# Linear attention with a per-step decay, then a two-layer network, on one core: idle products, conversions and transposes placed anew in rounds 0 and 1

## Chip, core and metric

The kernel runs on one core of a Trainium2 chip. The metric is the time of the program on the device in microseconds (us), the median of several executions. Five engines take part: TensorE (PE, matrix products and transposes into PSUM), VectorE (DVE), ScalarE (ACT), GpSimd (POOL) and SyncE (SP, which issues most DMAs). Each follows its own list of instructions, in order, and waits on semaphores for the others.

## What is computed

Inputs r, k, v, w have the shape (4, 8, 768, 48): batch, heads, steps, width. For each batch and head a 48 by 48 state runs over 768 steps; the outputs of the heads are put side by side (width 384), normed, and sent through two dense layers with a residual.

```python
for t in range(S):
    cur = einsum('bhd,bhe->bhde', u[None] * kt, vt)
    y[:, :, t] = einsum('bhd,bhde->bhe', rt, state + cur)
    state = wt[:, :, :, None] * state + einsum('bhd,bhe->bhde', kt, vt)
x = y.transpose(0, 2, 1, 3).reshape(B, S, H * D)
mu = mean(x); var = mean((x - mu) ** 2)
xn = (x - mu) / sqrt(var + 1e-6) * g_ln
out = x + maximum(xn @ w_ch1, 0) @ w_ch2        # 384 -> 1536 -> 384
```

## The kernel before, in words

**Tiling.** The work is cut into 8 rounds, each one batch and one half of 384 steps. A round has two units of four heads; u0, u1 are the units of round 0, units 2 and 3 those of round 1, and so on. Inside a unit two heads stand on the partitions (a pair, `pr`), and steps are cut into chunks of 64.

**Attention in levels.** Within a chunk the decay between two steps is built up by doubling. There are six levels (`NLEV`). At level `lev`, `quads` (line 366) makes the level products a_ps (24 products of fp32, each two PE instructions, so 48 per unit), `grow` (386) multiplies blocks of r and k in place by decays (DVE, one operation for each of r and k), and `keep` (401) copies the wanted part of a_ps into A (DVE, predicated copies; after the last level ACT copies, run later by `finish`, line 423). `quads` of the next level reads what `grow` wrote. `turned` (276) transposes w, k or r of one pair: three PE transposes into one PSUM buffer (w_ps, k_ps, r_ps) and one ACT copy out (to wT, kT, rT). The buffers are those of pool `ps_t`, two in all, which `product_sums` (own_ps), `ends` (kn_ps) and `turned_x` (xT_ps) share in turn: a third user waits until the first one's copy on ACT is done. `totals` (293) makes products of decays on DVE. `products` and `product_sums` make each step's own term with u. After the levels `ends` transposes k, `states` makes kv on PE and runs the state over the chunks on DVE, and `outputs` makes y.

**The network's weights.** w_ch1 and w_ch2 come in 24 raw parts of 384 KB, and both are rewritten once. `fetch` asks for a raw part by DMA (four buffers). `begin` is the first half of a conversion: three ACT operations (into w_sb, and twice into a buffer "held" or "rest"), after which it fetches the next raw part. `join` is the second half, three DVE operations. Parts from 12 on have four rest buffers, which ACT writes and join frees.

**The network's products.** `mlp` (562) is a generator: a step is six PE instructions of 384 columns, either one h_ps with a relu on ACT or a part of o_ps. `fill(until, tasks)` (line 619) spreads a slot's tasks evenly between the MLP steps up to a running total. A slot is one level of one round, and its totals stand in `UNTIL`.

**Idle products.** `warm(n)` issues n products of zeros, 128 by 128 (named "idle"), into a PSUM buffer that nobody reads; each is two PE instructions.

**Order.** The names PE, ACT, DVE, POOL and SPO (lines 67 to 69) keep the program's order on their engines. So an ACT copy that stands behind a conversion in the program runs behind it, and a DMA on SPO behind those before it. Loads on plain SP may be placed by the scheduler.

**Round 0** (lines 648 to 721) is written out by hand: transposes of u0 and u1, level 0, loads of round 1 and of v, two conversions (`begin`, lines 669 and 670), then levels 1 to 5 (674 to 688) with the transposes of round 1 between them, nine PE transposes a level from level 2 on (list `ahead`). A third conversion stands in level 1 and a fourth in level 3. Three more come with `own_term`, `outputs` and `norm`, after the levels. **Round 1** (line 731 on, `rnd == 1`) has no attention of an earlier round to finish; it has the levels of units 2 and 3, the first MLP steps, 17 begins and 21 joins (`BEGINS`, `JOINS`, line 730), and the transposes of round 2 in slots 1 to 3. In its slot 5 joins and begins stand first among the tasks, then `ends` and `finish`.

## Time and profile before

| what | us |
|---|---|
| median of 11 runs | 601.7 |
| lowest, highest | 597.5, 604.92 |
| profiled execution, its own time | 602.64 |
| its span, first to last instruction | 600.9 |
| PE busy | 578.9 |
| DVE busy | 294.8 |
| ACT busy | 199.7 |
| mean granted clock of TensorE | 0.969 |

The profile is of one execution. The span runs from the first to the last instruction; the program's own time has 1.74 us more around it. Each group is a line of the program's helper that keeps the order (L49 everywhere), so groups are told apart by the tiles they read and write: "a_ps<-rT,kT" are level products. "Idle before" is the time an engine stood before a group, and the name behind the arrow is what it waited for. A granted clock of 0.50 means that TensorE ran at half speed in that stretch; a busy PE at half speed still counts as busy.

The conversions of round 0 on ACT, with the copies around them, as the timeline has them (start, duration in us, what):

| start | us | ACT |
|---|---|---|
| 16.50 | 0.90 | two copies of k of u1 |
| 17.29 | 3.19 | conversions 0 and 1, to 20.48 |
| 22.33 | 0.17 | copy of own_ps of u1 |
| 23.94 | 1.69 | conversion 2, after a wait of 1.44 for its raw part |
| 25.88 | 1.12 | two copies of w of unit 2 |
| 32.75 | 1.67 | conversion 3 |

### The profile page before, as it was taken

What the parts mean: (1) busy time and instruction counts of PE and PEld (TensorE: products, weight loads), DVE (VectorE), ACT (ScalarE), POOL (GpSimd) and SP (SyncE); (2) the same over time, 40 slices, a digit from 0 to 9 for tenths busy, and PEclk for the clock granted to TensorE, in tenths of its full rate; (3) what the DMA queues carried; (4) which work ended last, traced back from release to release, by engine and by line L of the source; (5) the groups of instructions that cost most, each with busy time, mean ns of one, the idle gap of its engine ahead of it and who ended that gap; (6) DMA issues with size and microseconds to landing.
All of it is one profiled execution on the core that took longest, in us unless ns stands there. A gap on an engine that the chain in (4) does not pass through costs nothing.

```text
span 600.9 us, 19140 instructions
## 1 busy us (share of the span) xinstructions
PE 578.9 (96%) x8550; PEld 395.1 (66%) x8550; DVE 294.8 (49%) x706; ACT 199.7 (33%) x430; POOL 70.0 (12%) x100
## 2 busy tenths in 40 slices
PE   8997979899999999999999999999999999999997
PEld 7887656566666766676666666667666666666554
DVE  3857968989546554435265344526245332130000
ACT  3547766812352215411343215321241015301200
POOL 5000000002170007000240007000230000000000
PEclk9659889999999999999999999999999999999999
DMA  9972697134432412132113402012000000000000
GB/s 158 191 181 76 159 231 181 52 66 89 89 62 51 95 38 41 34 78 59 32 24 61 94 16 54 1 32 58 15 2 4 15 14 14 2 14 26 0 14 26
DMA packets 122129, 36.82 MB, mean 61 GB/s; under 512 B 115776, under 2 KB 118976, under 8 KB 122048
## 3 DMA queue, kind: packets, MB, share of 16 engines
q1 hardware_dynamic: 119648, 35.31, 26.7%
q8 instruction: 67, 1.10, 0.8%
q10 hardware_dynamic: 2400, 0.30, 0.6%
q14 instruction: 14, 0.11, 0.1%
HBM read 28.51 MB, written 4.72 MB: 55 GB/s over the span
## 4 chain that ended last, share of the span: by engine, by line
PE 86%; ACT 5%; DVE 5%; issue 2%; DMA 1%; SPq 0%; DVEq 0%; ACTq 0%
PE h_ps L49 29%; PE o_ps L49 29%; PE a_ps L49 11%; PE y L49 4%; PE r_ps L49 2%; PE w_ps L49 2%; PE k_ps L49 2%; PE kv L49 2%; PE xT_ps L49 2%; PE kn_ps L49 2%; DVE w_sb L49 1%; PE own_ps L49 1%; ACT rest L49 1%; DVE A L49 1%; PE idle L49 1%
## 5 line engine op out<-in xcount | busy, mean ns | idle before, releaser
L49 PE MATMUL o_ps<-w_sb,h 128*128 128x384 f32 x576 | 199.5, 492 | 0.5 <-issue 0.5
L49 PE MATMUL h_ps<-xT,w_sb 128*128 128x384 f32 x576 | 197.7, 494 | 0.0
L49 PEld LDWEIGHTS h_ps<-xT,w_sb 128*128 128x128 f32 x576 | 107.0, 193 | 65.9 <-issue 2.1
L49 PEld LDWEIGHTS o_ps<-w_sb,h 128*128 128x128 f32 x576 | 105.4, 192 | 63.0 <-issue 2.9
L49 PEld LDWEIGHTS a_ps<-rT,kT 48*64 48x64 f32 x4608 | 78.4, 142 | 20.5 <-issue 15.7
L49 PE MATMUL a_ps<-rT,kT 48*64 48x32 f32 x4608 | 83.5, 226 | 7.3 <-issue 5.6
L49 ACT ACTIVATE h<-h_ps 128x384 f32<-128x384 f32 x96 | 46.5, 489 | 124.9 <-PE h_ps L49 124.8
L49 DVE TENSOR_TENSOR o<-o_ps,x 128x384 f32<-128x384 f32 x24 | 13.4, 557 | 133.5 <-PE o_ps L49 133.5
L49 POOL TENSOR_TENSOR vo<-v,own 128x576 f32<-128x576 f32 x12 | 14.3, 1195 | 366.5 <-DVE own L49 366.5
L49 DVE COPY_PREDICATED A<-mask,a_ps 128x384 f32<-128x384 int8 x80 | 54.4, 750 | 0.0
L49 DVE TENSOR_TENSOR rT<-rT,tot 128x384 f32<-128x384 f32 x80 | 45.6, 579 | 15.5 <-PE a_ps L49 15.5
L49 DVE TENSOR_TENSOR kT<-kT,tot 128x384 f32<-128x384 f32 x80 | 45.3, 567 | 10.7 <-PE a_ps L49 10.2
L49 DVE SCALAR_TENSOR_TENSOR s<-s,decay,kv 128x48 f32<-128x48 f32 x160 | 29.3, 258 | 28.1 <-PE kv L49 28.1
L49 DVE TENSOR_TENSOR x<-y,vo 128x288 f32<-128x288 f32 x32 | 13.2, 454 | 50.1 <-PE y L49 50.1
L49 ACT ACTIVATE xT<-xT_ps,g_sb 128x384 f32<-128x384 f32 x24 | 13.7, 580 | 58.6 <-PE xT_ps L49 58.5
L49 ACT COPY rT<-r_ps 128x384 f32<-128x384 f32 x32 | 14.4, 480 | 43.8 <-PE r_ps L49 43.8
L49 ACT COPY kT<-k_ps 128x384 f32<-128x384 f32 x32 | 14.8, 480 | 38.1 <-PE k_ps L49 38.1
L49 PEld LDWEIGHTS y<-v,A 64*64 64x64 f32 x384 | 20.9, 134 | 8.2 <-issue 6.0
L49 PE MATMUL y<-v,A 64*64 64x48 f32 x384 | 23.9, 222 | 0.8 <-DVE A L49 0.8
L49 PE MATMUL y<-vx,A 64*64 64x48 f32 x384 | 23.9, 222 | 0.0
L49 ACT COPY kn<-kn_ps 128x384 f32<-128x384 f32 x32 | 14.4, 480 | 28.3 <-PE kn_ps L49 28.2
L49 PE MATMUL y<-sx,rx 48*64 48x48 f32 x384 | 23.3, 219 | 0.0
(70 smaller groups left out, 551.9 us busy)
## 6 DMA issues: line engine op xcount, KB each, us to landing
raw<-in_moe_w_ch_dram SPq DMA_DIRECT2D x24, 384.0 KB, 4.0
nat_w<-in_w_dram SPq DMA_DIRECT2D x48, 96.0 KB, 2.9
nat_k<-in_k_dram SPq DMA_DIRECT2D x48, 96.0 KB, 2.9
v<-in_v_dram SPq DMA_DIRECT2D x48, 96.0 KB, 3.0
out_dram<-o SPq DMA_DIRECT2D x24, 192.0 KB, 1.9
nat_r<-in_r_dram SPq DMA_DIRECT2D x45, 96.0 KB, 3.0
vx<-v SPq DMA_DIRECT2D x32, 72.0 KB, 2.3
nat_r<-in_r_dram ACTq DMA_DIRECT2D x3, 96.0 KB, 3.9
```

Of the source, the lines that this page charges most:

```text
L49: return lambda *args, **kw: self.tc.keep_in_program_order(f(*args, **kw))
```

## The change

It does five things:

1. In round 0 it adds idle products: two before `product_sums(u0)`; two instead of one after r and after k of u1; three before level 1; two between the level products of u0 and u1 in level 1; and 3, 2, 1, 1, 3 at the end of the product part of levels 1 to 5, where only level 5 had two. That is 17 more.
2. It puts four conversions ahead of level 1, where two stood, and takes those of levels 1 and 3 away. The DMAs that they ask for (raw parts 4 and 5) now stand on SP before the loads of v, and parts 6 and 7 before those of vx.
3. In round 1 the begins of the six slots are 3, 2, 3, 3, 4, 2 (before 4, 3, 1, 3, 4, 2) and the joins 3, 3, 3, 3, 4, 5 (before 3, 3, 3, 4, 4, 4).
4. The transposes of round 2 are spread over slots 0 to 3 as 2, 4, 4, 2 pairs (before 0, 4, 6, 2), in the order w, k, r.
5. The new helper `mixed` spreads the begins, joins and transposes of a slot evenly over one list. That list is added at the end of the slot's tasks, so in slot 5 it comes after `ends` and `finish`. The total of MLP steps after slot 2 is 9 instead of 8.

```diff
+    def mixed(*lists):
+        return [
+            t for _, t in sorted(
+                (((i + 0.5) / len(l), t) for l in lists for i, t in enumerate(l)),
+                key=lambda at: at[0],
+            )
+        ]
...
     totals(0, DVE)
+    warm(2)
     product_sums(u0)
     for nm in "rk":
         run(each(turned, [u1], nm, pairs))
-        warm(1)
+        warm(2)
...
     load(new[1], eng=SPO)
-    run(each(load_v, [u0, u1], [SPO]) + each(load_vx, [u0, u1], [SPO]))
     begin()
     begin()
+    run(each(load_v, [u0, u1], [SPO]))
+    begin()
+    begin()
+    run(each(load_vx, [u0, u1], [SPO]))
+    warm(3)
     grow(u1, 0)
     keep(0, 0)
...
     for lev in range(1, NLEV):
-        for q in (u0, u1):
-            quads(q, lev)
+        quads(u0, lev)
+        if lev == 1:
+            warm(2)
+        quads(u1, lev)
         if lev == 1:
             product_sums(u1)
         else:
             run(ahead[3 * lev - 6 : 3 * lev - 3])
-        if lev in (1, 3):
-            begin()
-        if lev == 5:
-            warm(2)
+        warm((3, 2, 1, 1, 3)[lev - 1])
...
-    UNTIL = [3, 6, 8, 11, 14, 16, 19, 21, 24]
+    UNTIL = [3, 6, 9, 11, 14, 16, 19, 21, 24]
...
-    JOINS, BEGINS = (3, 3, 3, 4, 4, 4), (4, 3, 1, 3, 4, 2)
+    ahead = [t for nm in "wkr" for t in each(turned, units_of(2), nm, pairs)]
+    JOINS, BEGINS = (3, 3, 3, 3, 4, 5), (3, 2, 3, 3, 4, 2)
...
-                for i in range(max(JOINS[lev], BEGINS[lev])):
-                    tasks += [join] * (i < JOINS[lev]) + [begin] * (i < BEGINS[lev])
...
-            if new and first <= lev < first + 3:
-                due = each(turned, new, "wkr"[lev - first], pairs)
-                if rnd == 1 and lev == 2:
-                    due += each(turned, new[:1], "r", pairs)
-                if rnd == 1 and lev == 3:
-                    due = due[NP:]
-                tasks += due
+            if rnd > 1 and new and first <= lev < first + 3:
+                tasks += each(turned, new, "wkr"[lev - first], pairs)
...
+            if rnd == 1:
+                n = (1, 2, 2, 1, 0, 0)[lev] * NP
+                tasks += mixed([begin] * BEGINS[lev], [join] * JOINS[lev], ahead[:n])
+                del ahead[:n]
             fill(UNTIL[slot], tasks)
```

## The prediction

> **What bounds the kernel now.** I read the page first, then the granted clock in fine windows, then the timeline of each engine where the clock falls, and last the chain of waits.

> The page says that TensorE (PE) bounds the whole, and that the first slices differ from the rest:

> ```profile
> PE 578.9 (96%) x8550; PEld 395.1 (66%) x8550; DVE 294.8 (49%) x706; ACT 199.7 (33%) x430; POOL 70.0 (12%) x100
> PEclk9659889999999999999999999999999999999999
> ```

> From slice 7 on hardly anything but PE work counts, and the change doesn't touch it: whatever is won or lost in the first 125 us goes through to the end. In the first slices the clock is low though PE is busy. Windows put at the edges of the clock's steps show it (name, PE busy, PEld, DVE, ACT, POOL, clock, DMA share, GB/s):

> ```profile
> 20.62:44.50 23.88, 23.88 (x440) 20.97 (x439) 16.57 (x33) 9.58 (x20) 0.00 (x0) 0.50 0.84 192
> 58.17:65.00 6.83, 6.30 (x27) 4.62 (x27) 6.35 (x15) 3.54 (x7) 0.00 (x0) 0.50 0.73 159
> 78.65:82.06 3.41, 3.28 (x10) 2.35 (x11) 1.29 (x4) 1.41 (x4) 0.00 (x0) 0.50 1.02 335
> ```

> Half clock for 23.9 us: that is all of levels 2 to 5 of round 0. The timeline of PE there:

> ```profile
> 22.22 2.79 PE L49 MATMUL a_ps<-rT,kT 48*64 48x32 f32 x96
> 24.94 1.54 PE L49 MATMUL w_ps<-ident,nat_w 128*128 128x128 f32 x6
> 26.41 0.90 PE L49 MATMUL r_ps<-ident,nat_r 128*128 128x128 f32 x3
> 27.24 2.79 PE L49 MATMUL a_ps<-rT,kT 48*64 48x32 f32 x96
> ```

> A level takes 5.02 us of PE at half clock (2.72 for 96 level products, 2.30 for 9 transposes). VectorE (DVE) needs four growths at 0.48 apart and two predicated copies of about 0.47, 2.9 us, and waits ("1.76 <-PE a_ps" at 38.86). The other stretch is round 1:

> ```profile
> PE w_ps L49 <- ACT wT L49: 2.8, 1, 2.8
> PE a_ps L49 <- DVE s L49: 1.2, 1, 1.2
> ```

> At 75.99 the third w transpose needs a PSUM buffer whose copy stands on ScalarE (ACT) behind conversions: ACT is full from 66.1 to 79.1. PE idles 2.79, and the clock is then half for one window.

> [...] the steps stand at 20.62, 44.50, 58.17, 65.00, 78.65, 82.06 and 464.32, all multiples of 3.41 apart to within 0.03. So the phase differs from execution to execution; the 11 times spread over 7.4 us. [...] here window 78.65 to 82.06, half of it w transposes, raised it, so I count them. [...] "ACT own" at 22.33 stands where the program has it, before the third conversion. [...]

> **What the clock asks for (my estimate).** I weigh each product by the part of the array that it uses: two idle products of 128 columns took 0.22 us, so an a_ps product (32 columns, 48 by 64 of 128 by 128) counts 0.005 us, a call of quads (48) 0.24; a y or kv product 0.010; own_ps (2 columns) nothing; a transpose 0.125. Windows that ended in half clock: 17.20 to 20.62 (144 a_ps) 21%; 54.75 to 58.17 27%; 75.24 to 78.65 22%; the one before 464.32 29%. Windows that kept full clock: 47.90 to 51.30 35%, 51.30 to 54.75 39%. So the bound lies near a third. To come back, 79% (24.03 to 27.45 and 34.27 to 37.69) did not do and 96% (78.65 to 82.06) did.

> **The change part by part.**

> *Idle products.* 17 more: at 13.2 two (they lie beside the wait of own_ps for wT, 0.24: about 0.1 is late), one more each after r and k (0.22 each, the second behind k; the growth chain of u1 moves by about 0.3), three and two around the level-1 products, then 3, 2, 1, 1, and 3 instead of 2. Each costs 0.21 at full clock and 0.43 at half. The first aim is met: window 17.20 to 20.62 now holds 1.07 of idle products besides 0.8 of quads, about 56%, and full clock stays past 20.6.

> *Four conversions ahead of the levels.* Before, two stood there, the third after the copy of own, the fourth in level 3. ACT runs in order: the third needs raw part 2, and the fourth raw part 3. The SP queue is unchanged up to that fetch: part 2 was issued at 19.66 and landed at 23.94 (ACT's wait shows it), part 3 was issued at 21.2 and landed about 4.0 later, 25.2. So ACT stands from 20.5 to 23.94, converts until 25.6 and, at 1.56 a conversion, until 27.15; only then comes the copy of own_ps (0.17). own_ps holds one of the two ps_t buffers. In level 2, PE does its first w transpose in the other, and the second waits for this copy, with the r transpose, the idle products and level 3 behind it. With quads of level 2 done at about 24.3 (own_ps 20.7 to 22.2, three idle products, quads from 22.9), PE idles from 24.65 to 27.3. This is the wait of 75.99 at a new place. Window 24.03 to 27.45 then holds about 18%, and the clock falls after all, at 27.45 or (20.62 to 24.03 holds 30%) at 24.03.

> *Then the levels at half clock.* Second w transpose 27.3 to 28.0, r to 28.8, two idle products 0.85: quads of level 3 at 29.6 instead of 27.31, +2.3. Levels 3, 4 and 5 have 1, 1 and (3-2) more idle products at 0.43: +1.3. kn_ps begins at 46.8 instead of 43.23: **+3.6**. From there all recurs one clock window (3.41) later, so I add nothing. Bounds: if the clock returns in 37.69 to 41.10 (transposes plus idle products fill 87% there, between the two known values) this is +1.3; if the wait is bridged at full clock, see the first rival.

> *Raw parts ahead of v.* Parts 4, 5 are issued at 28.2 and 6, 7 after v, where they came at 35.9. Four took about 4.3 us of the DMA (38 to 42 at 252 to 396 GB/s). v lands at about 35.3, vx at about 41; kv needs v at 45.78 and y needs vx at 50.60. The slack covers it: nothing. Without it, it would be at most the 4.3. The w loads of round 2 behind them on SP move little.

> *Round 1.* Conversions are 3, 2, 3, 3, 4, 2 instead of 4, 3, 1, 3, 4, 2; the w transposes of the first unit come in slot 0. The first conversion of slot 0 now lies before the first relu, in ACT's idle 63.1 to 65.76. ACT per level is then about 7 us against 8 of PE: the 2.79 goes, with 1.7 of the 3.41 at half clock and some of 0.30, 0.19 and 0.41. What is late next: in slot 5 the kn transposes now stand ahead of all conversions and of the first MLP step. Before, o_ps 109.17 to 111.21 covered the growth of k (DVE 110.20 to 111.2). DVE's load is the same, and one join moves from slot 3 to slot 5. DVE by my count: level 2 begins at 80.65 instead of 84.08, level 3 at 89.1, level 4 at 96.0, the growth of k at 104.9 to 105.9 (before 110.2 to 111.2); PE ends its level-5 quads at about 103.2. So PE waits 2.7 there, after which the clock falls in most phases (1.7). Sum on PE from 62.28 to the a_ps of 120.17: 57.9, less waits of 4.9 and 1.7 of clock, is 51.3 of work; after, 51.3 + 2.7 + 0.3 + (0 to 1.7) = 54.3 to 56.0: a gain of 1.9 to 3.6. DVE, which ends its joins at 114.3 instead of 118.19, allows 3.9. I take **-2.8**.

> *Step 9 for 8 in UNTIL* moves one MLP step from slot 3 to 2: no work, in the sum above.

> Sum: 602.64 (the profiled execution; span 600.9) + 3.6 - 2.8 = 603.4; it lay 0.94 above the median of 601.7, so the median comes to 602.5.

> **Rivals.**

> 1. *Full clock through round 0.* If no window over the wait at 24.65 falls under a third, quads of level 3 start at 28.6, and a level takes about 2.9: kn_ps at 37.5, -6.0 with its own products at full clock. With -2.8 this is 593.8, median about 593. For: 56% in the first window. Against: 2.6 us idle of 3.41; by my weights only some 0.65 of 3.41 of the phases pass both windows.
> 2. *Half clock, but raised in level 4:* +1.3 - 2.8, median 600.2, or lower where it is raised in level 3: 598. For: 87% lies between 79 and 96; against: the window must hold the whole run of 2.73.
> 3. *The wait of round 1 moves to level 5 and gives all back (slower).* DVE's joins are the same 21, and the chain of waits over 101 to 118 is ACT conversions and DVE joins in turn. If DVE reaches the growth of k no earlier than 110, PE waits 5 where an o_ps step stood, and round 1 gives 0: 602.64 + 3.6 = 606.2, median 605.3. It decides from a wait of 4.9. Against: DVE idled 4.0 and 1.6 in levels 2 and 3, which earlier level products remove.

> **How the numbers follow.** Likeliest case 0.43, 602.5, its own range 600 to 604.6; rival 1 0.23; rival 2 0.14, half of it under 598.7; rival 3 0.20. A measurement here tells about 0.5% (3 us) from no change. Faster: 0.23 + 0.07 = 0.30; within: 0.43 + 0.07 = 0.50; slower: 0.20. The range 594 to 606 leaves out half of rival 1 and the tail of rival 3.

> **What would show it.** A PE wait "w_ps <- ACT" or the like of over 2 us at about 25 and ACT's own copy at about 27 show the block; a clock of 0.5 from about 27.4 to 48 and level products 5.4 apart show the half-clock levels. Clock 1.00 over 25 to 40 makes it wrong by 9 us. In round 1 the wait at 76 must be gone and one before kn_ps of about 2.7 be there; were it absent, round 1 gains a further 2 to 3.

## The result, and the profile after

The changed kernel takes 609.93 us (median of 12 runs, 606.65 to 614.62). The kernel before took 601.7 (47 runs beside them). The ratio is 1.0153 with a 95% interval of 1.0123 to 1.0183: slower by 1.5%, where 602.5 and "no change" were forecast. Medians are of all executions; ratios, and the means further down, leave out those that took over 1.5% more than the fastest of their kernel. The profiled execution of the changed kernel took 614.57 us, the second longest of the 12; its span is 612.8 and its mean clock 0.961 (before 602.64, 600.9, 0.969). So its profile shows more loss than the median has.

Busy times and the clock row of the page of the changed kernel, the counterparts of the two page lines shown of before:

```profile
PE 584.4 (95%) x8584; PEld 399.3 (65%) x8584; DVE 295.5 (48%) x706; ACT 198.9 (32%) x430; POOL 70.4 (11%) x100
PEclk9877899779999999999999999989999899999999
```

PE has 34 matrix instructions more (17 idle products of two) and 5.5 us more of busy time. Before, the clock row had its low digits, 6 and 5, in the second and third place; now there is no digit below 7, but 7 and 8 stand in two places, and 8 further on. Windows put at the edges of the clock's steps give the stretches (columns as in the windows of before):

```profile
20.00:25.50 5.50, 4.24 (x121) 3.84 (x117) 5.50 (x12) 1.95 (x4) 0.00 (x0) 1.00 1.01 228
25.50:35.70 10.20, 8.76 (x155) 7.92 (x157) 3.54 (x8) 4.13 (x10) 0.00 (x0) 0.50 0.81 180
42.60:46.00 3.40, 2.79 (x13) 2.82 (x14) 1.12 (x3) 0.96 (x2) 0.00 (x0) 0.50 0.33 63
52.80:63.00 10.20, 10.20 (x256) 9.82 (x256) 5.09 (x13) 4.64 (x11) 0.00 (x0) 0.50 0.32 87
...
107.40:114.20 6.80, 6.11 (x10) 3.20 (x10) 2.78 (x7) 3.64 (x8) 0.00 (x0) 0.50 0.26 72
127.90:134.70 6.80, 6.50 (x102) 4.87 (x103) 6.37 (x22) 1.72 (x4) 0.00 (x0) 0.50 0.01 4
```

With the window left out (66.5 to 69.9) the stretches at 0.50 up to 135 us are six, of together 40.8 us, against 34.1 in three before. Cut to 0.01 us, the stretches from step to step between 25.50 and 134.73 last 10.24, 6.83, 3.41, 6.83, 10.24, 3.41, 3.42, 37.54, 6.83, 13.65 and 6.83 us, each at 0.50 or at 1.00 throughout: multiples of 3.41 to within 0.03, as in the forecast's profile. A clock window is one length of 3.41 between such steps; that its filling decides on the clock behind it is the forecast's estimate. The first falls, at 25.50 here and at 20.62 before, are 4.88 apart, which is no multiple of 3.41. The level products of level 5 of round 0 and most of level 4's now run at full clock, but own_ps and y of round 0 (52.8 to 63.0) and two stretches around the end of round 1 do not.

The waits of PE (in total, number, longest; us):

```profile
PE o_ps L49 <- ACT h L49: 4.2, 1, 4.2
PE a_ps L49 <- issue: 3.8, 3, 1.7
PE w_ps L49 <- ACT own L49: 2.7, 1, 2.7
PE k_ps L49 <- DMA vx<-v: 2.6, 1, 2.6
PE a_ps L49 <- DVE s L49: 2.5, 1, 2.5
```

The wait of 2.8 for wT in round 1 is gone, as forecast. A wait for own is there, as forecast. The largest, 4.2 for h, was in no step of the forecast. Round 0 on the timeline of PE (start, duration, what, idle before and its releaser):

```profile
23.70 0.55 PE L49 MATMUL w_ps<-ident,nat_w 128*128 128x128 f32 x3
26.94 0.90 PE L49 MATMUL w_ps<-ident,nat_w 128*128 128x128 f32 x3 [2.70 <-ACT own L49]
...
29.26 2.79 PE L49 MATMUL a_ps<-rT,kT 48*64 48x32 f32 x96
...
38.50 1.60 PE L49 MATMUL a_ps<-rT,kT 48*64 48x32 f32 x96
...
43.21 1.51 PE L49 MATMUL k_ps<-ident,nat_k 128*128 128x128 f32 x6 [2.63 <-DMA vx<-v]
...
45.80 0.91 PE L49 MATMUL kn_ps<-ident,kT 128*128 128x128 f32 x6
```

and on that of ACT:

```profile
23.30 0.57 ACT L49 ACTIVATE w_sb<-raw 128x384 f32<-128x384 f32 x1 [4.07 <-DMA raw<-in_moe_w_ch_dram]
...
26.74 0.14 ACT L49 COPY own<-own_ps 128x12 f32<-128x12 f32 x1
```

This is the block that the forecast describes: ACT stands 4.07 for raw part 2, the copy of own_ps comes at 26.74, and PE's second w transpose waits 2.70 for it. At the end of round 0 kn_ps begins at 45.80 (before 43.02 in this view; the forecast set 46.8 against 43.23).

Now round 1. First PE of the kernel before at the end of level 4, then PE, ACT and DVE of the changed kernel around level 4 and level 5:

```profile
103.47 4.24 PE L49 MATMUL o_ps<-w_sb,h 128*128 128x384 f32 x12
```

```profile
103.08 0.81 PE L49 MATMUL o_ps<-w_sb,h 128*128 128x384 f32 x2
108.09 6.53 PE L49 MATMUL o_ps<-w_sb,h 128*128 128x384 f32 x10 [4.21 <-ACT h L49]
...
128.20 2.79 PE L49 MATMUL a_ps<-rT,kT 48*64 48x32 f32 x96 [2.47 <-DVE s L49]
```

```profile
103.46 0.52 ACT L49 ACTIVATE w_sb<-raw 128x384 f32<-128x384 f32 x1
106.48 1.22 ACT L49 ACTIVATE rest<-raw 128x384 int32<-128x384 uint32 x2 [2.50 <-DVE w_sb L49]
107.57 0.47 ACT L49 ACTIVATE h<-h_ps 128x384 f32<-128x384 f32 x1
```

```profile
101.53 0.55 DVE L49 TENSOR_TENSOR rT<-rT,tot 128x384 f32<-128x384 f32 x1
...
103.41 1.02 DVE L49 COPY_PREDICATED A<-mask,a_ps 128x384 f32<-128x384 int8 x2
104.34 0.75 DVE L49 TENSOR_TENSOR vo<-v,own 128x576 f32<-128x576 f32 x1
105.01 0.74 DVE L49 TENSOR_SCALAR w_sb<-w_sb 128x384 f32<-128x384 f32 x2
105.89 0.56 DVE L49 CUSTOM_DVE_ANT_0 w_sb<-w_sb,rest 128x768 uint16<-128x768 uint16 x1
...
115.52 1.26 DVE L49 TENSOR_TENSOR kT<-kT,tot 128x384 f32<-128x384 f32 x2 [4.99 <-PE a_ps L49]
```

Before, the twelve o_ps products run in one piece. Read the three of the changed kernel from the bottom up. A rest buffer is freed by a join on DVE. The join that frees one stands behind DVE's growths, predicated copies and own term of level 4 and starts at 105.01. ACT has begun a conversion at 103.46, needs a rest buffer for its second part and stands 2.50. The relu of the MLP step (h at 107.57) is queued behind it. The pool of h_ps and o_ps (`ps_m`) has two PSUM buffers, and the second o_ps product needs the one that this relu empties; so PE stands 4.21, until the relu ends. Half clock begins at 107.4, so the ten o_ps products take 6.53. Since the level-5 products come behind them, DVE in turn idles 4.99, and the state chain of round 1 ends later against PE: a_ps of round 2 waits 2.47 for s (before 1.19). Before, the longest wait of ACT for a join from 84 to 118 us was 0.55.

From the first h_ps product to the first a_ps of round 2, round 1 took 60.3 us (67.88 to 128.20) against 57.9 before; the first h_ps came 5.6 later than before (62.27).

### The profile page after: what moved, and what is told of

Its sections match the earlier page's. It is cut to its first block, busy times and chain, and to the rows that moved or that the text cites. A ratio compares the mean times of both kernels' runs of the same rounds, so it can differ in the third digit from the quotient of the medians.

```text
span 612.8 us, 19202 instructions
## 1 busy us (share of the span) xinstructions
PE 584.4 (95%) x8584; PEld 399.3 (65%) x8584; DVE 295.5 (48%) x706; ACT 198.9 (32%) x430; POOL 70.4 (11%) x100
## 4 chain that ended last, share of the span: by engine, by line
PE 86%; ACT 4%; DMA 3%; DVE 3%; issue 2%; POOL 1%; SPq 1%; DVEq 0%; POOLq 0%
PE o_ps L49 31%; PE h_ps L49 30%; PE a_ps L49 10%; PE y L49 4%; PE k_ps L49 2%; PE kv L49 2%; PE r_ps L49 2%; PE w_ps L49 2%; DMA vx<-v 1%; PE xT_ps L49 1%; PE kn_ps L49 1%; DMA raw<-in_moe_w_ch_dram 1%; PE own_ps L49 1%; DMA v<-in_v_dram 1%; ACT rest L49 1%
## 5 line engine op out<-in xcount | busy, mean ns | idle before, releaser
L49 PE MATMUL o_ps<-w_sb,h 128*128 128x384 f32 x576 | 204.8, 503 | 4.2 <-ACT h L49 4.2
L49 PE MATMUL h_ps<-xT,w_sb 128*128 128x384 f32 x576 | 196.7, 490 | 0.0
L49 PEld LDWEIGHTS o_ps<-w_sb,h 128*128 128x128 f32 x576 | 108.5, 197 | 69.3 <-issue 6.3
L49 PEld LDWEIGHTS h_ps<-xT,w_sb 128*128 128x128 f32 x576 | 105.9, 191 | 64.0 <-issue 0.6
L49 PEld LDWEIGHTS a_ps<-rT,kT 48*64 48x64 f32 x4608 | 77.4, 140 | 19.6 <-issue 14.5
L49 PE MATMUL a_ps<-rT,kT 48*64 48x32 f32 x4608 | 82.6, 224 | 6.3 <-issue 3.8
L49 ACT ACTIVATE h<-h_ps 128x384 f32<-128x384 f32 x96 | 46.6, 490 | 118.3 <-PE h_ps L49 118.1
L49 DVE TENSOR_TENSOR o<-o_ps,x 128x384 f32<-128x384 f32 x24 | 13.4, 557 | 134.3 <-PE o_ps L49 134.2
L49 POOL TENSOR_TENSOR vo<-v,own 128x576 f32<-128x576 f32 x12 | 14.3, 1194 | 377.7 <-DVE own L49 375.4
L49 DVE COPY_PREDICATED A<-mask,a_ps 128x384 f32<-128x384 int8 x80 | 54.4, 750 | 0.0
L49 DVE TENSOR_TENSOR rT<-rT,tot 128x384 f32<-128x384 f32 x80 | 45.6, 578 | 14.6 <-PE a_ps L49 14.6
L49 DVE TENSOR_TENSOR kT<-kT,tot 128x384 f32<-128x384 f32 x80 | 45.4, 567 | 14.0 <-PE a_ps L49 13.1
L49 DVE SCALAR_TENSOR_TENSOR s<-s,decay,kv 128x48 f32<-128x48 f32 x160 | 29.3, 258 | 28.1 <-PE kv L49 28.1
L49 DVE TENSOR_TENSOR x<-y,vo 128x288 f32<-128x288 f32 x32 | 13.1, 453 | 55.5 <-PE y L49 55.5
L49 ACT ACTIVATE xT<-xT_ps,g_sb 128x384 f32<-128x384 f32 x24 | 13.7, 581 | 59.8 <-PE xT_ps L49 59.8
L49 ACT COPY kT<-k_ps 128x384 f32<-128x384 f32 x32 | 14.9, 479 | 42.8 <-PE k_ps L49 42.8
L49 ACT COPY rT<-r_ps 128x384 f32<-128x384 f32 x32 | 14.4, 478 | 42.5 <-PE r_ps L49 42.5
L49 PEld LDWEIGHTS y<-v,A 64*64 64x64 f32 x384 | 22.7, 144 | 7.4 <-issue 6.2
L49 PE MATMUL y<-vx,A 64*64 64x48 f32 x384 | 26.0, 232 | 0.0
L49 PE MATMUL y<-v,A 64*64 64x48 f32 x384 | 26.0, 232 | 0.0
L49 ACT COPY kn<-kn_ps 128x384 f32<-128x384 f32 x32 | 14.2, 481 | 34.0 <-PE kn_ps L49 34.0
L49 PE MATMUL y<-sx,rx 48*64 48x48 f32 x384 | 25.2, 229 | 0.0
```

The lines of the kernel that those rows point to most:

```text
L49: return lambda *args, **kw: self.tc.keep_in_program_order(f(*args, **kw))
```

## The experiments

The theory after the result (**A**): in round 1, `mixed` puts a begin ahead of the join where two stand at the same place in the list, while the loop that it replaces put the join first. So two begins of slot 4, where one stood, come ahead of the relu. With one join fewer in slot 3 as well, the begins of slot 4 run out of rest buffers; the wait for h, and the half clock after it, follow. Rival **B**: the loss is round 0's, where ACT's conversions hold the copy of own, and round 1 only inherits a delay. Rival **C**: no single wait matters; what counts is which clock windows are full enough, and the two parts move them.

All ratios are against runs of the kernel before on the same chip. Medians of two sets of runs are compared by their ratio only, since the kernel before had a median of 601.7 in one set and 603.24 in another.

**e1, round 1 alone.** Round 0 as before; `UNTIL`, `JOINS`, `BEGINS`, `mixed` and `ahead` as changed.

> Round 0 as before, round 1 as changed. Theory A (the order inside slot 4 of round 1 puts a conversion that waits for a rest buffer ahead of the relu on ACT, and PE stands 4.2 us behind it): slower than before by 2 to 5 us, with a PE wait of about 4 us for the copy h by ACT and half clock after it. Rival B (round 1 is a gain of 2 to 3.6 us as forecast, all of the loss is in round 0): 598 to 600 us, no such wait.

Measured: 606.83, ratio 1.0065 (1.0033 to 1.0098); its profile has the wait "o_ps <- ACT h" of 4.2 and the wait for s of 2.5.

**e2, round 0 alone.** Idle products and conversions of round 0 as changed, round 1 as before.

> Round 0 as changed, round 1 as before. Theory A (round 0 loses by the copy of own that stands behind the third and fourth conversion, and the clock that falls in that wait): +3 to +6 us over before, the PE wait of 2.7 us for the copy of own at about 25 to 27 us. Rival B (all of the loss is in round 1): within 2 us of before.

Measured: 605.39, ratio 1.0048 (1.0021 to 1.0076), with the wait of 2.7 for own. So each part alone loses, and B holds for less than half of the loss. The product of the two ratios is 1.0113; the whole change is at 1.0153. The intervals leave room for a difference of 0.4% and for none.

**e3 and e4, the two halves of round 0.** e3 has the idle products only, e4 the conversions and the order of the loads only:

```diff
e3:
+    warm(2)
     product_sums(u0)
...
+        if lev == 1:
+            warm(2)
...
+        warm((3, 2, 1, 1, 3)[lev - 1])
e4:
-    run(each(load_v, [u0, u1], [SPO]) + each(load_vx, [u0, u1], [SPO]))
     begin()
     begin()
+    run(each(load_v, [u0, u1], [SPO]))
+    begin()
+    begin()
+    run(each(load_vx, [u0, u1], [SPO]))
...
-        if lev in (1, 3):
-            begin()
```

> Only the 17 idle products are added; conversions, raw parts and round 1 as before. Theory A (idle products keep the clock when ACT does not block the transposes): clock 1.00 over 21 to 40 us in most executions, first h_ps 5 to 7 us earlier, time 3 to 7 us under before. Rival C (idle products are pure cost): +3.6 (17 at 0.21) to +7.3 us (at 0.43).

> Only the four conversions ahead of the levels and the order of raw parts, v and vx; no added idle products, round 1 as before. Theory A: half clock from about 20.6 us as before, and the wait for the copy of own costs 1 to 2 us (level-3 products at 28.8 instead of 27.3): +1 to +2.5 us. Rival C (the conversions are free because half clock hides them): within 1 us of before.

Measured: e3 603.85, ratio 1.0018 (0.9995 to 1.0042); e4 603.6, ratio 1.0021 (0.9997 to 1.0046). Neither half is clear of no change by itself. In e4's profile the 2.7 for own is there. In e3's there is no such wait, PE is full, and the clock fell in the levels all the same (windows of e3):

```profile
20.30:23.70 3.40, 3.40 (x95) 3.24 (x98) 3.40 (x7) 0.17 (x1) 0.00 (x0) 0.99 0.70 140
23.70:40.70 17.00, 17.00 (x344) 15.15 (x339) 9.70 (x19) 7.50 (x15) 0.00 (x0) 0.50 0.79 165
```

PE is busy for the whole of the window from 20.3 to 23.7, and it ends in half clock: it holds own_ps, whose products have two columns. By the weights of the forecast (48 level products ahead of own_ps, three idle products and about 24 level products behind it) it is about 30% full; that is an estimate, and lies under the forecast's bound of a third. So the block on ACT isn't the only thing that lets the clock fall here.

**f1, the order in `mixed`.** e1 with joins first:

```diff
-                tasks += mixed([begin] * BEGINS[lev], [join] * JOINS[lev], ahead[:n])
+                tasks += mixed([join] * JOINS[lev], [begin] * BEGINS[lev], ahead[:n])
```

> Round 0 as before; round 1 as changed, but in each slot the join goes ahead of the begin with which it ties, so that only one conversion of slot 4 stands ahead of the relu on ACT. Theory A (the waiting second conversion ahead of the relu is what costs in round 1): the PE wait of 4.2 us for h by ACT is gone, 3.5 to 7 us under the round-1 change alone, so 0 to 3 us under before; a wait of about 2.7 us before kn_ps takes its place in part. Rival B (the total work of DVE bounds round 1, the wait only moves): within 1.5 us of the round-1 change alone.

Measured: 602.4, ratio 0.9994 (0.9957 to 1.003). The wait for h is gone. But ACT still waits for a rest buffer, only now behind the relu (ACT timeline of f1):

```profile
100.65 0.46 ACT L49 ACTIVATE h<-h_ps 128x384 f32<-128x384 f32 x1
101.50 0.56 ACT L49 ACTIVATE w_sb<-raw 128x384 f32<-128x384 f32 x1 [0.39 <-DMA raw<-in_moe_w_ch_dram]
103.66 1.24 ACT L49 ACTIVATE rest<-raw 128x384 int32<-128x384 uint32 x2 [1.60 <-DVE w_sb L49]
```

What stands in the PE timeline of f1 instead of the wait for h:

```profile
108.23 3.01 PE L49 MATMUL kn_ps<-ident,kT 128*128 128x128 f32 x12 [2.05 <-DVE kT L49]
...
121.27 2.48 PE L49 MATMUL a_ps<-rT,kT 48*64 48x32 f32 x96 [2.31 <-DVE s L49]
```

The first is the wait before kn that the forecast has (2.7 there), the second is one that it lacks: the state chain on DVE starts behind the last joins, and these stand for the last two begins, which the new order of slot 5 puts behind the copies of `ends` and `finish` on ACT (DVE timeline of f1):

```profile
116.16 0.76 DVE L49 TENSOR_SCALAR w_sb<-w_sb 128x384 f32<-128x384 f32 x2 [1.83 <-ACT w_sb L49]
```

Its profile is at half clock over 108.0 to 111.5 and 121.7 to 128.5.

**f2, the list ahead of the ends in slot 5.** f1 with `tasks = mix + tasks` in slot 5, which gives back the cover that kn had.

> As the run with the join first, and in slot 5 the list of joins and begins stands ahead of the kn transposes, as it did before the change. Theory A: the wait before kn_ps goes, 1 to 3 us under the run with the join first. Rival B (the end of round 1 is set by the joins and the states on DVE): no difference beyond 1 us.

Measured: 602.28, ratio 1.002 (0.9994 to 1.0046), so no gain over f1. The wait for s is gone, and the wait before kn moved: kn's copies on ACT now stand behind the conversions (PE timeline of f2).

```profile
113.90 1.54 PE L49 MATMUL kn_ps<-ident,kT 128*128 128x128 f32 x6 [4.13 <-ACT kn L49]
```

**g1, the whole change with joins first.** The one line of f1 in the changed kernel.

> The whole change, with one thing undone: in a slot of round 1 the join goes ahead of the begin with which it ties. Theory A (the order is worth some 4 us in the whole change too): 604 to 606.5 us, 3.5 to 6 under the change, no PE wait of 4 us for h by ACT. Rival D (round 0 and round 1 act on one another, and the rest of the loss stays): over 607.

Measured: 606.35, ratio 1.0033 (1.0002 to 1.0063). This line takes 1.2% (1.0153 to 1.0033) off the whole change. With joins first the two parts multiply to 1.0042 (f1 times e2), so nothing is left over there; if the 0.4% above is real, it goes with the order.

**g2, the joins of before with begins first.** e1 with `JOINS` 3, 3, 3, 4, 4, 4, so one join comes back into slot 3.

> Round 0 as before, round 1 as changed with begin ahead of join, but the joins of the slots as before (3, 3, 3, 4, 4, 4), so that slot 4 begins with one rest buffer more free. Theory A1 (what costs is that the conversion ahead of the relu waits for a rest buffer): ACT's wait of 2.5 us for a join is gone and the PE wait for h falls from 4.2 to under 2 us, 2 to 4 us under the round-1 change alone. Theory A2 (two conversions ahead of the relu cost by their own 3.1 us, waiting or not): PE wait still over 3 us, within 1.5 us of the round-1 change alone.

Measured: 606.51, ratio 1.0058 (1.0027 to 1.0088). The wait for h is halved (PE timeline of g2), and the time is not shown to be better than e1's (1.0065).

```profile
100.12 3.49 PE L49 MATMUL o_ps<-w_sb,h 128*128 128x384 f32 x10 [1.95 <-ACT h L49]
```

In g2's profile ACT's wait for a rest buffer (1.50) stands behind the relu, and the 1.95 that is left is the length of the two conversions ahead of it. So by these profiles some 2.3 of the 4.2 come from the buffer and the rest from a second conversion ahead of the relu. The times don't tell the two apart: the wait is as A1 has it, the time as A2 has it. What is shown to cost is the order of begin and join; that the count in slot 3 costs isn't shown.

**g4, the begins alone.** The kernel before with `BEGINS` 2, 3, 3, 3, 4, 2.

> The kernel before with begins 2, 3, 3, 3, 4, 2 instead of 4, 3, 1, 3, 4, 2 and nothing else: fewer conversions ahead of the w copies of slot 1. Theory A (the first wait of round 1 is worth its 2.8 us and the clock window after it): the PE wait for wT is gone, 2 to 4 us under before. Rival B (DVE bounds round 1, the wait moves to its end): within 1 us of before.

Measured: 604.5, ratio 1.0023 (0.9997 to 1.0049). So A's gain didn't come. The profile (of an execution of 608.86, one of its longest) has two PE waits of 1.8, for wT and for kT, in place of one of 2.8.

f4a and f4b test the forecast's estimate of a bound near a third. By its weights the end of round 0 lies under it (27% over 54.75 to 58.17), and so does the window over own_ps in level 1 (about 30%, e3).

**f4a, idle products at the end of round 0.** The kernel before with `warm(5)` between the states of u0 and of u1 and `warm(9)` for `warm(2)` ahead of xT.

> The kernel before with 5 more idle products between the states of u0 and u1 and 9 instead of 2 before the transposes of xn, both where PE waits anyway. Theory A [...]: clock 1.00 from about 44 to 76 us, first h_ps 2 to 4 us earlier, time 2 to 4 us under before. Rival C (idle products cost what they take): +1 to +2.6 us.

Measured: 600.99, ratio 0.9975 (0.9949 to 1.0002): a gain of 1.5 us that isn't clear of none.

**f4b, idle products in the levels, and own_ps out of them.** f4a, with the idle products of the change in the levels (7, 2, 1, 1 and 1 at the ends of levels 1 to 5), `product_sums(u1)` moved from level 1 to level 5, and the third conversion from level 1 to 2:

```diff
...
-            product_sums(u1)
-        else:
+            warm(2)
+        quads(u1, lev)
+        if lev > 1:
...
-        if lev in (1, 3):
+        if lev in (2, 3):
             begin()
         if lev == 5:
-            warm(2)
+            product_sums(u1)
+        warm((7, 2, 1, 1, 1)[lev - 1])
```

> As the run before it, and in the levels of round 0: the idle products of the change with 7 at the end of level 1, the own products of u1 (own_ps[...]) moved from level 1 to level 5, the third conversion moved from level 1 to level 2. Theory A [...]: no half clock over 20 to 45 us, first h_ps 6 to 9 us earlier than before the change, time 6 to 9 us under before. Rival C (the clock falls for another reason): half clock of 10 us or more in 20 to 45, time within 3 us of before.

Measured: 595.14, ratio 0.9867 (0.9813 to 0.9921), of six executions. The profiled one is the longest of them (601.18) and is at half clock over 29.1 to 49.6, so the profile doesn't show what A says of 20 to 45; by span and mean clock the other five have 3.5 to 17.9 us at half clock in all.

**g3, f4b with the begins of g4.**

> The run with the levels and the end of round 0 filled (own_ps of u1 in level 5, third conversion in level 2, idle products where PE waits), and in round 1 the begins 2, 3, 3, 3, 4, 2. Theory A: the two gains add, 8 to 11 us under before. Rival B (round 1 takes nothing): 6 to 8 us under before.

Measured: 597.44, ratio 0.9917 (0.9881 to 0.9953): not shown to be better than f4b.

**h1, f1 with idle products in round 1.** Nine ahead of kn in slot 5 and eight ahead of the first level products of round 2, each group waiting where PE would have stood.

> As the run with the join first on round 0 as before, and idle products where PE waits: 9 ahead of the kn transposes of slot 5 and 8 ahead of the first level products of round 2. Theory A (the half clock after the two waits eats the gain of round 1): no half clock over 105 to 130 us, 1.5 to 4 us under the run with the join first, so 598 to 601 us. Rival B (DVE is late whatever the clock): within 1 us of the run with the join first, or up to 1 us over.

Measured: 603.99, ratio 1.0023 (0.9998 to 1.0049). In its profile there is no half clock between 65.2 and 130 and the wait for s is 0.7, and yet it is not faster than f1: A failed here. The profile isn't like the other executions in this: over the whole run they spend 1.0 us more at half clock than the kernel before, on the mean (table below).

**h2, f4b's round 0 with h1's round 1.**

> The filled round 0 (own_ps of u1 in level 5, third conversion in level 2, idle products where PE waits) and the round 1 of the other run of this call. Theory A: both gains add, 8 to 11 us under before, 591 to 594 us. Rival B: 5 to 8 us under before, as with the filled round 0 alone.

Measured: 591.19 (590.71 to 592.99), ratio 0.9828 (0.9789 to 0.9867). This is the fastest, 1.7% ahead of the kernel before (five executions). The windows from 0 to 125 us, first of h2, then of before, then of the changed kernel:

```profile
0.00:125.00 125.00, 118.09 (x2318) 91.87 (x2319) 100.00 (x244) 75.27 (x162) 8.69 (x38) 1.00 0.72 153
```

```profile
0.00:125.00 125.00, 114.11 (x1963) 87.96 (x1964) 94.35 (x232) 76.45 (x162) 8.69 (x38) 0.86 0.67 148
```

```profile
0.00:125.00 125.00, 109.92 (x1890) 85.48 (x1891) 87.06 (x204) 73.17 (x157) 9.07 (x38) 0.86 0.68 148
```

h2 runs 125 us at full clock and gets 2318 matmuls through (96 of them are its 48 added idle products), before 1963, the changed kernel 1890. The last two have the same clock, 0.86; the changed kernel loses there by waits (4.2 us less PE work).

**Clock and waits told apart over all runs (theory C).** Every execution in the sets of e1 to h2 has its span and mean granted clock, so its time at half clock is 2 x (1 - clock) x span, if the clock is 0.50 or 1.00 throughout, as in the stretches above. Over 183 executions of the kernel before, the time follows it: 588.8 + 0.34 x (us at half clock), correlation 0.85; the time at half clock runs from 27 to 52 us, with a median of 38.5. That is a correlation, not an experiment; but nothing was changed between those executions. If 0.34 is the price in the other kernels too, the mean difference of each from the kernel before, in the set beside it, divides into a part by the clock and a rest (waits and added products). The set beside the changed kernel has no clocks; there the mean of the 183 stands in.

| kernel | mean difference, us | us at half clock, difference | by the clock | rest |
|---|---|---|---|---|
| changed kernel | +9.2 | +7.1 | +2.4 | +6.8 |
| e1 round 1 alone | +3.9 | +6.4 | +2.1 | +1.7 |
| e2 round 0 alone | +2.5 | -7.9 | -2.7 | +5.2 |
| e3 idle products alone | +1.3 | -9.1 | -3.1 | +4.3 |
| e4 conversions alone | +1.2 | 0.0 | 0.0 | +1.2 |
| f1 join first | -0.5 | +3.9 | +1.3 | -1.8 |
| f2 list first | +1.3 | +6.6 | +2.2 | -0.9 |
| h1 f1 and idle products | +1.3 | +1.0 | +0.3 | +1.0 |
| f4b | -6.7 | -26.9 | -9.1 | +2.3 |
| h2 | -10.4 | -36.3 | -12.2 | +1.9 |

The rests of e1 and f1 are 3.5 apart, near to the wait of 4.2 that f1 hasn't. The rest of e3, 4.3, is near to 17 products at 0.21, 3.6. So the idle products of the change buy 9.1 us less at half clock, worth 3.1, and cost at least as much. C has by this about a quarter of the loss of the change (2.4 of 9.2), and more than the whole gain of f4b and h2.

## Why the prediction was wrong

**The step that failed is the -2.8 of round 1.** The forecast put the order of conversions and relus on ACT at nothing. Measured alone (e1) it is +0.65%, 3.9 us of 602 (2.0 to 5.9). The forecast checked ACT's load per level (7 us against PE's 8) and DVE's total, and followed the wait that would go. It didn't follow the order within a slot: how many begins stand ahead of a relu, and which join frees the rest buffer that such a begin needs. In the changed kernel two begins stand there, the second waits 2.50 for its buffer, and PE waits 4.21 for the relu. That order decides: joins first takes e1 from 1.0065 to 0.9994, and the whole change from 1.0153 to 1.0033.

**Even with the order mended the -2.8 is not shown: f1 is at 0** (-2.6 to +1.8 us). The schedule of the forecast came true up to the wait before kn: put on the time scale of before (2.67 us less, by the first h_ps), f1's growth of k starts at 104.95 (104.9 in the forecast), its level-5 products end at 103.5 (103.2), and the wait is 2.05 (2.7). The wait for wT in round 1 went. Two terms were wrong. DVE ends its joins at 116.6 on that scale and not at 114.3, since it stands 1.83, 0.38 and 0.30 for the last two begins; so a_ps of round 2 waits 2.31 for the states, against 1.19 before. And there is more half clock, 3.9 us on the mean, 1.3 us by the price above, of which the forecast had 0 to 1.7. In f1's profile round 1 takes 56.3 us, 1.6 less than before, near the 54.3 to 56.0 of the forecast; over its executions no gain is shown. Rival 3 (the gain of round 1 is given back) has this as its outcome, though from a wait of 4.9 at kn, and none such came; so its mechanism wasn't right either. Why h1, without these waits and half clocks in its profile, wins nothing over f1 stays open: its 17 idle products cost about 3.6 us where they are not beside a wait, and on the mean they took only 2.9 us of half clock away (1.0 by the price).

**Round 0, +3.6 forecast, +2.9 measured (e2; +1.3 to +4.6): the block was right, the size in part luck.** In the profile of the change own's copy was forecast at about 27 and found at 26.74; level 3 at 29.6, found at 29.26; PE's wait 2.65, found 2.70; kn_ps at 46.8, found at 45.80. Wrong was the length of the half clock. It ended at 35.7, in level 4, as rival 2 had it (0.14); the likeliest case kept it through the levels. The window before (32.3 to 35.7) is by the forecast's weights about 81% full (2.4 us of transposes and idle products, the rest level products), which these weights can't tell from the 79% that didn't do. What the full clock won, the wait of 2.63 ahead of k_ps at 43.21 took. In e2's profile, with the same round 0, kn_ps began at 43.03, no later than before, and the first h_ps 2.8 late (65.07), behind half clock from 49.9 to 60.1. And on the mean of e2 the table has 2.7 us won by the clock and 5.2 lost by waits and products, where the forecast had the clock no better than before.

**"Full clock stays past 20.6": right in the profile of the change. That the block makes the clock fall: not shown to be needed.** There the clock fell at 25.50, at the end of a window with the wait in it. But e3 falls at 23.66 without the wait. The forecast had named this as well: the window over own_ps holds 30%, and the clock may fall at 24.03. In f4b own_ps leaves level 1, its place is filled, and the end of round 0 is filled too (which alone, f4a, isn't clear of no gain): of 37 us at half clock on the mean it loses 27. That is what the estimate would have it, though f4b moves more than this one window.

**"All recurs one clock window later, nothing added": wrong in the profile of the change.** own_ps and y met the half clock for three windows (52.8 to 63.0, against 58.17 to 65.00 before), and the first h_ps was 5.6 late where kn_ps was 2.8 late. Over e2's executions half clock is not a loss on the mean: they have 7.9 us less of it than before.

**Raw parts ahead of v, "nothing": not contradicted.** v landed 5.2 and vx 6.2 us after issue, and the profile puts the wait of 2.63 at 43.21 down to vx. But it stands at a count of PE instructions at which PE also stalls with nothing to wait for, and it ends like those stalls (last section). e2 has the same loads, and at the same count only a stall of 0.32.

**The price of an idle product** (0.21 at full clock) was about right: six PE instructions, three products, took 0.67 us in e3, and seven products 1.75 in f4b (0.22 and 0.25 each). e3's 9.1 us less half clock bears out that they count for the clock. PE's busy time alone doesn't tell the clock: in h2 PE is busy for 118.09 of 125 us and the clock is 1.00 throughout, but in e3's window at 20.30 PE is busy for all 3.40 us, with products of two columns among them, and the clock is 0.50 from 23.66 on. The change could hardly be forecast to better than some us: the kernel before varies by 11 us from execution to execution, and most of that goes with its half clock (correlation 0.85).

Of the result's 1.5%, then: some 0.65% is round 1 alone and 0.5% round 0 alone, both shown; the 0.4% between their product and the whole is within the intervals, and nothing here tells whether it is real.

## What to carry to other kernels

When work of two engines is laid out anew, follow each buffer and not only each engine's load: for every "get a buffer" write down which instruction frees it, what stands ahead of that on its engine, and what is queued behind the one that waits. At equal places in a merged list, put the half that frees ahead of the half that takes, and count how many of the latter come ahead of work that another engine waits for: here putting the joins first, with one conversion fewer ahead of a relu, took the whole change from 1.0153 to 1.0033. Where the granted clock falls though PE is busy, look first whether the 3.41 us ahead of the fall hold nearly empty products, as in e3, where own_ps with its two columns stands ahead of the fall at 23.66. Here filling around it brought about what it cost (e3), and moving own_ps out, with its place filled, went with a gain of 1.3% (f4b).

## What was not expected of the hardware

```profile
q8 instruction: 67, 1.10, 0.8%
```

67 packets for 17,168 PE instructions, matmuls and weight loads, are one for 256 (each is 16 KB, 1.10 MB in 67); that they carry PE's instructions is inferred from this ratio. In the records of this queue in the two traces, each of the nine stalls ends 1.26 to 1.58 us after a packet of it has landed. The wait of 2.63 at matmul 730, put down to vx, leaves 0.73 and ends 1.46 us after such a packet (41.75, PE at 43.21), so it fits these stalls. That a stall waits for its packet is an inference from counts and times; no run here changed it. Nor is it shown whether such a stall bears on the clock: in f4b's profile one of 1.42, to 28.01, lies within the 3.41 us before half clock begins (29.1); in h2 the stall ahead of the same level products is 0.45, to 27.97, and the clock stayed at 1.00.
